# A gated S5 and SiLU-FFN layer on one core: C by DMA transposes, state slot 3 in pairs, four conversions on GpSimd

## The chip, the cores and the metric

The kernel runs on one core of one Trainium2 chip. The metric is the device time of one execution in microseconds. Before the change the median of three runs is 145.91 us (145.41 to 146.05). All times below are microseconds unless marked otherwise; times within an execution count from its first instruction.

## What is computed

One input `x` of 2048 tokens by 448 features goes through two branches, and a sigmoid gate per token mixes them. Branch A is a diagonal complex state-space layer (S5) with 448 states, branch B a feed-forward layer with 1792 hidden features:

```
g     = sigmoid(sum(x * gate_w))
Lbar  = exp(dt * Lam);  dt = exp(log_dt);  Lam = Lambda_re + i Lambda_im
Bu    = x @ (((Lbar - 1) / Lam)[:, None] * (B_re + i B_im)).T
h_t   = Lbar * h_{t-1} + Bu_t                 (over 2048 tokens)
a     = 2 * real(h @ (C_re + i C_im).T) + x * Dskip
b     = silu(x @ w1) @ w2
out   = g * a + (1 - g) * b
```

Inputs and output are bf16.

## The kernel before

**Chunks and slots.** Tokens are worked on in four chunks of 512 (`CH`), the readout in 16 blocks of 128 tokens. The 448 complex states make 896 real rows, kept in seven slots of 128 partitions: slots 0 to 2 hold the real parts of 384 states, 4 to 6 their imaginary parts, and slot 3 the real parts of the last 64 states above their imaginary parts. Before, the 384 states of slots 0 to 2 are interleaved (state 3p + s stands in partition p of slot s), so that a load of B reads three neighbouring rows of DRAM into each partition; C's columns and the parameters are then taken with a stride of 3.

**The complex scan as a real one.** `lanes(tc)` turns each chunk's inputs U by the phase of every state and time (products with COS and SIN on DVE), runs a real scan with decay `rc` on DVE for each slot (L670), converts each result Gf to bf16 (Gb, L673, on ScalarE, ACT below) and turns it back (products at L657), which gives H for the readout. A slot's partner is the slot 4 away; slot 3's partner is its own other half, which a DMA within SBUF swaps into row 7 of U and Gb (`swapped`, L636; in chunk 0 two DVE copies, L653, for U). COS and SIN of 512 times are made at the start for four blocks of states: the phase is multiplied by the time (L493 on ACT for blocks 0 and 1, L496 on GpSimd for 2 and 3), brought into the range of the sine by subtracting the nearest whole turn (`nearest`, `minus`, DVE), and put through ACT's sine. Eight columns of sines at the end of a chunk (s8, c8, L524 to L526) serve the carry between chunks (CC, SS, gin) and, over a row of small GpSimd instructions (L529), the scales `sc1` and `sc2` that turn C into the scaled readout weights CP.

**PE's work.** TensorE (PE) multiplies x by B for U (`bu_pair`, and `bu_last` for slot 3, L644), by w1 for the hidden layer (`ffn1_pair`), the hidden layer by w2 (`ffn2`, L706), and H by CP (`readout`, L731). The contraction over 448 features is 3.5 times 128. `step` takes two outputs at once, one fed from the upper 64 rows of the array and one from the lower: seven matmuls of half height for each output, in a `begin` of 8 and an `end` of 6 (L595). The end of a pair is issued after the begin of the next. `bu_last` does slot 3 with four matmuls of full height, the last padded with zeros (L799). ACT or DVE empties the result from one of eight PSUM banks: U (L622, L624), the SiLU (L695), Tb = (1 - g) b (L710). DVE adds the branches up in `readout` (tf at L725, ot at L734), and a DMA on SyncE's queue (SP) writes each block of 128 rows.

**The start and C.** x of chunk 0, B and C come as they lie in DRAM and are transposed by PE with the identity matrix (L435, L569, L747), x of chunks 1 to 3 by DMA transposes (L369). PE runs 15 idle matmuls (L420) while x arrives. The parameters (Lambda, log_dt, gate_w: `prm`, four rows) are copied once by DVE (L453) and brought into columns by PE (L459, L461).

**Order.** Engines issue in order. PE's order is the order of the calls at the end of the kernel, written out by hand. For the other engines and the DMA queues a planner (`Plan.order`) simulates the program with a cost and a priority for each operation and picks the next one that could start. `Waits` turns the dependences into semaphore waits. PSUM banks are handed out by the planner too.

Of the kernel before, what the change touches and what calls it, by code (L numbers as in the profile page):

```python
# [7 lines left out]
ALU = mybir.AluOpType  # L8
# [253 lines left out]
def bass_gated_mix__ssm_conv_s5__dense_activation_silu__prompt_kernel(nc, A_x, A_Lambda_re, A_Lambda_im, A_B_re, A_B_im, A_C_re, A_C_im,  # L262
               A_log_dt, A_Dskip, B_x, B_w1, B_w2, gate_w, out):
    with ExitStack() as ctx:
# [25 lines left out]
        Cnat = Tb[0:112, 7:16, :].rearrange("p a b -> p (a b)")[:, 0:3840].rearrange("p (b l) -> p b l", b=4)  # L290
# [13 lines left out]
        prm = sb("prm", [4, 512], BF16)  # L304
# [68 lines left out]
        load("sp", Bnat[:, 0:3, :], A_B_re[0:384, :].rearrange("(p s) d -> p s d", s=3), "Bn0", 384 * 896, 1)  # L373
        load("sp", Bnat[:, 4:7, :], A_B_im[0:384, :].rearrange("(p s) d -> p s d", s=3), "Bn3", 384 * 896, 2)
# [12 lines left out]
        load("sp", Cnat[:, :, 0:448], A_C_re.rearrange("(b p) l -> p b l", p=112), "Cn0", 448 * 896, 11)  # L387
        load("sp", Cnat[:, :, 576:960], A_C_im[:, 0:384].rearrange("(b p) l -> p b l", p=112), "Cn1", 448 * 768, 12)
        load("sp", Cnat[:, :, 448:512], A_C_im[:, 384:448].rearrange("(b p) l -> p b l", p=112), "Cn2", 448 * 300, 13)
        load("sp", Cnat[:, :, 512:576], A_C_re[:, 384:448].rearrange("(b p) l -> p b l", p=112), "Cn3", 448 * 300, 14)  # L390
# [36 lines left out]
        def x_transposes(n):  # L427
            tk = Ps()

            def mm(pe):  # L430
                for q in range(2):
                    i = 2 * n + q
                    for b in range(4):
                        o = (q * 4 + b) * 128
                        r = pe.transpose(bk16(tk)[:, o:o + 128], xnat[:, b, XCOL[i]:XCOL[i] + 128], ident[:, :])  # L435
                return r
            P.add("pe", mm, ["xn0", "ident"], [tk], 0.5)
            if n == 0:
                DVE(lambda e: e.tensor_copy(xT[:, 0:2, 0:CH], bk16(tk)[:, :].rearrange("p (q n) -> p q n", q=2)),
                    [tk], ["xT00"], 0.7, 2)  # L440
            else:
                ACT(lambda e: e.activation(xT[:, 2, 0:CH], bk16(tk)[:, 0:CH], AF.Copy), [tk], ["xT01"], act_cost(512), 1)
                DVE(lambda e: e.tensor_copy(xT[:, 3, 0:CH], bk16(tk)[:, CH:2 * CH]), [tk, "xT01"], ["xT02"], 0.42, 2)

        x_transposes(0)
        x_transposes(1)

        def xr(tc):
            return [f"xT{tc}{k}" for k in range(2 if tc else 3)]


        prmn = [f"prm{k}" for k in range(4)]
        DVE(lambda e: e.tensor_copy(prm[:, 448:512], prm[:, 384:448]), prmn, ["prmd"], 0.2, 1)  # L453
        tk = Ps()

        def prm_t(pe, tk=tk):
            for b in range(4):
                lanes = prm[0:4, b:384:3] if b < 3 else prm[0:4, 384:512]
                pe.transpose(bk16(tk)[:, 4 * b:4 * b + 4], lanes, ident[0:4, 0:4])  # L459
            for b in range(3):  # L460
                r = pe.transpose(bk16(tk)[:, 16 + 4 * b:16 + 4 * b + 4], prm[0:4, 128 * b:128 * b + 128], ident[0:4, 0:4])  # L461
            return r
        P.add("pe", prm_t, prmn + ["prmd", "ident"], [tk], 0.3)
        DVE(lambda e, tk=tk: e.tensor_copy(
            pc[:, :, :], bk16(tk)[:, 0:16].rearrange("p (b k) -> p k b", k=4)), [tk], ["pc"], 0.2, 1)
        DVE(lambda e, tk=tk: e.tensor_copy(
            gwc[:, 0:3], bk16(tk)[:, 16:28].rearrange("p (b k) -> p k b", k=4)[:, 3, :]), [tk], ["gwc"], 0.2, 4)
        POOL(lambda e: e.tensor_copy(gwc[:, 3:4], pc[:, 3, 3:4]), ["pc"], ["gwc3"], 0.2, 15)
# [20 lines left out]
        for b in range(4):  # L489
            q = b % 2  # L490
            dst = Gf[:, b, :]
            if b < 2:
                ACT(lambda e, b=b, dst=dst: e.activation(dst, itf[:, :], AF.Copy, scale=ph[:, b:b + 1]),  # L493
                    ["itf", "ph"], [f"Gf{b}"], act_cost(512, 1), 2)
            else:
                POOL(lambda e, b=b, dst=dst: e.tensor_single_scalar(dst, itf[:, :], ph[:, b:b + 1], ALU.mult),  # L496
                     ["itf", "ph"], [f"Gf{b}"], 1.65)
            DVE(nearest(wk[q], dst), [f"Gf{b}"], [f"Gf{4 + q}"], dve_cost(512, 2), 3)
            DVE(minus(dst, dst, wk[q]), [f"Gf{b}", f"Gf{4 + q}"], [f"Gf{b}"], dve_cost(512), 3)
# [59 lines left out]
        def b_transposes(slots, reads, h, to_act):  # L559

            tk = Ps()
            n = len(slots)

            def mm(pe):
                for q in range(2):
                    i = 2 * h + q
                    for j, s in enumerate(slots):
                        o = (q * n + j) * 128
                        r = pe.transpose(bk16(tk)[:, o:o + 128], Bnat[:, s, XCOL[i]:XCOL[i] + 128], ident[:, :])  # L569
                return r  # L570
            P.add("pe", mm, reads + ["ident"], [tk], 0.06 * 2 * n)
            dst = BT[:, 2 * h:2 * h + 2, slots[0] * 128:(slots[-1] + 1) * 128]
            src = lambda: bk16(tk)[:, 0:2 * n * 128].rearrange("p (q m) -> p q m", q=2)
            name = f"BT{h}_{slots[0]}"
            if to_act:
                ACT(lambda e: e.activation(dst, src(), AF.Copy), [tk], [name], act_cost(256 * n), 0)
            else:
                DVE(lambda e: e.tensor_copy(dst, src()), [tk], [name], 0.1 + 0.00058 * 256 * n, 0)

        B01, B23, B456 = (0, 1), (2, 3), (4, 5, 6)  # L580
        b_transposes(B01, ["Bn0"], 0, False)
        b_transposes(B01, ["Bn0"], 1, True)
        idle(2)
        b_transposes(B456, ["Bn3"], 0, False)
        b_transposes(B456, ["Bn3"], 1, True)
        b01, b23, b456 = ([f"BT{h}_{s}" for h in range(2)] for s in (0, 2, 4))
# [4 lines left out]

        def half_steps(pe, w, xc, a, b, lo, hi, start):
            for i in range(len(lo)):
                for p0, (tk, c0), k in ((0, a, lo[i]), (64, b, hi[i])):
                    r = pe.matmul(bk(tk), w[p0:p0 + 64, k, c0:c0 + 128], xT[p0:p0 + 64, k, xc:xc + CH],  # L595
                                  start=(start and i == 0), stop=(not start and i == 2))
# [4 lines left out]
        def step(pair):  # L601

            w, tc, ca, cb, reads, evict = pair
            a, b = Ps("pair"), Ps("pair")
            xc = tc * CH
            begin = lambda pe: half_steps(pe, w, xc, (a, ca), (b, cb), (0, 1, 2, 3), (0, 1, 2, 3), True)
            end = lambda pe: half_steps(pe, w, xc, (b, cb), (a, ca), (0, 1, 2), (0, 1, 3), False)
            reads = reads + xr(tc)
            P.add("pe", begin, reads, [a, b], 0.87, rows=64)
# [8 lines left out]


# [6 lines left out]
        def bu_pair(tc, k):  # L626
            sa, sb_ = ((0, 1), (4, 5), (6, 2))[k]

            def evict(a, b):
                u_out(sa, a)  # L630
                u_out(sb_, b, tc == 0)
            return BT, tc, 128 * sa, 128 * sb_, (b01, b456, b456 + b23)[k], evict
# [5 lines left out]

        def bu_last(tc):
            tk = Ps()  # L640

            def mm(pe):
                for i in range(4):
                    r = pe.matmul(bk(tk), BT[:, i, 384:512], xT[:, i, tc * CH:(tc + 1) * CH],  # L644
                                  start=(i == 0), stop=(i == 3))
                return r
            P.add("pe", mm, b23 + ["BT3z"] + xr(tc), [tk], 0.87)
            u_out(3, tk)
            if tc:
                swapped(U, "U", 0)  # L650
            else:
                for k, p in ((0, 0), (1, 64)):
                    DVE(lambda e, p=p: e.tensor_copy(U[p:p + 64, 7, :], U[64 - p:128 - p, 3, :]),  # L653
                        ["U3"], [f"U7{'ab'[k]}"], dve_cost(512, 4), 2)
# [4 lines left out]
        def lanes(tc):  # L659
# [7 lines left out]
            for s in (3, 0, 4, 1, 5, 2, 6):  # L667
# [5 lines left out]
                ACT(lambda e, s=s: e.activation(Gb[:, s, :], Gf[:, s, :], AF.Copy), [f"Gf{s}"], [f"Gb{s}"], act_cost(512), 4)  # L673
# [18 lines left out]
        def ffn1_pair(tc, k):  # L692
            def evict(a, b):
                for tk, fb in ((a, k), (b, 7 + k)):
                    ACT(lambda e, tk=tk, fb=fb: e.activation(aT[tc % 2][:, fb, :], bk(tk), AF.Silu),  # L695
                        [tk, "tbl"], [f"aT{tc % 2}_{fb}"], act_cost(512), 3)
            part = 0 if k < 3 else 1
            return w1s, tc, 128 * k, 896 + 128 * k, [f"w1{part}{n}" for n in range(5)], evict

        def ffn2(tb):  # L700
# [3 lines left out]
            def mm(pe, tk=tk):  # L704
# [4 lines left out]
            P.add("pe", mm, ["w2"] + [f"aT{tc % 2}_{fb}" for fb in range(NFB)], [tk], 2.66)  # L709
            ACT(lambda e, tk=tk: e.activation(Tb[:, tb, :], bk(tk)[:, 0:D_MOD], AF.Copy, scale=g1[:, tb:tb + 1]),  # L710
                [tk, f"g1_{tc}"], [f"Tb{tb}"] + [f"{'B' if tb < 7 else 'C'}n{k}" for k in range(4)], act_cost(448, 1), 3)
# [8 lines left out]
        def readout(tb):  # L720
            tc, o = tb // 4, (tb % 4) * 128
            t0 = tb * 128
            tk = Ps("C")
# [174 lines left out]
```

## Time and profile before

| What | us |
|---|---|
| Median of the runs | 145.91 |
| Profiled execution, its own time | 145.11 |
| Its span, first to last instruction | 143.3 |
| Half-height matmuls on B (L595), 168 | 19.7 busy |
| Half-height matmuls on w1 (L595), 392 | 43.8 busy |
| Hidden layer by w2 (L706), 224 matmuls | 44.7 busy |
| Readout (L731), 112 matmuls | 23.1 busy |
| DVE scans (L670), 21 of chunks 1 to 3 | 25.8 busy |
| ACT conversions Gb (L673), 28 | 17.2 busy |
| GpSimd scalings of 512 columns (L496), 2 | 3.1 busy |

The granted TensorE clock is 1.0 in the whole execution. A group of the profile is named by line, engine, operation and tile; its busy time is the sum of the durations of its instructions. Matmuls are pipelined, so that the duration of one (0.38 us at L595) is longer than the distance from one to the next; distances are read from the chain of waits, which gives start, length and count of each stretch. DMA issues on SP and ACT are not counted as busy.

### The profile page before, as it was taken

The numbers are of one execution on the slowest core, as the hardware profiler recorded it, in microseconds if no ns is written. First come the engines' busy times: TensorE is split into PE (matmuls) and PEld (weight loads), VectorE is DVE, ScalarE is ACT, GpSimd is POOL, SyncE is SP. The second block draws the span as 40 slices with busy tenths as digits, with TensorE's granted clock in tenths as the row PEclk, the third lists the DMA queues.
The fourth block names the chain that finished last, engine by engine and source line by source line (L and its number), as shares of the span: only waits on it lengthen the run. The fifth ranks groups of instructions, "written<-read, shape, count | busy, mean of one in ns | idle before, by whom it ended". The sixth has DMA issues, their size and how long they took to land.

```text
span 143.3 us, 2726 instructions
## 1 busy us (share of the span) xinstructions
PE 138.5 (97%) x1076; PEld 69.3 (48%) x1076; DVE 123.9 (86%) x144; ACT 82.6 (58%) x154; POOL 25.3 (18%) x62
## 2 busy tenths in 40 slices
PE   6899999999999999999999999999999999999991
PEld 4744543444446654444555554444455555555550
DVE  0459979999999999999799999969479999889592
ACT  3298799799778466978921134978811344411100
POOL 7176960000601300023170000040000000000000
PEclk9999999999999999999999999999999999999999
DMA  4999979015987000000011002000020021000022
GB/s 145 311 252 263 327 140 236 2 37 121 180 204 250 5 0 19 17 0 5 0 39 64 20 17 69 0 0 5 0 69 32 0 73 32 32 18 16 32 92 71
DMA packets 18165, 11.44 MB, mean 80 GB/s; under 512 B 8036, under 2 KB 17896, under 8 KB 18152
## 3 DMA queue, kind: packets, MB, share of 16 engines
q1 hardware_dynamic: 18144, 11.27, 31.1%
q8 instruction: 8, 0.13, 0.4%
q14 instruction: 5, 0.04, 0.1%
q10 hardware_dynamic: 8, 0.00, 0.0%
HBM read 6.94 MB, written 1.84 MB: 61 GB/s over the span
## 4 chain that ended last, share of the span: by engine, by line
PE 91%; ACT 5%; DVE 2%; issue 0%; DVEq 0%
PE ps L595 37%; PE ps L706 30%; PE ps L731 15%; PE ps L644 3%; PE ps L420 2%; ACT aT L695 2%; ACT COS L512 1%; PE ps L569 1%; PE ps L747 1%; PE ps L770 1%; PE ps L435 1%; DVE Gf L482 0%; DVE ot L734 0%; ACT SIN L507 0%; DVE U L653 0%
## 5 line engine op out<-in xcount | busy, mean ns | idle before, releaser
L706 PE MATMUL ps<-w2s,aT 128*128 128x448 bf16 x224 | 44.7, 353 | 0.0
L595 PE MATMUL ps<-xT,w1s 64*128 64x512 bf16 x392 | 43.8, 376 | 0.3 <-ACT aT L695 0.3
L695 ACT ACTIVATE aT<-ps 128x512 bf16<-128x512 f32 x56 | 29.6, 598 | 5.1 <-PE ps L595 5.1
L706 PEld LDWEIGHTS ps<-w2s,aT 128*128 128x128 bf16 x224 | 21.7, 98 | 20.4 <-issue 0.4
L595 PEld LDWEIGHTS ps<-xT,w1s 64*128 64x128 bf16 x392 | 18.9, 94 | 23.5 <-ACT aT L695 1.6
L710 ACT ACTIVATE Tb<-ps,g 128x448 bf16<-128x448 f32 x16 | 10.1, 633 | 32.6 <-PE ps L706 26.6
L670 DVE TENSOR_TENSOR_SCAN Gf<-rc,gin,PA 128x512 f32<-128x512 f32 x21 | 25.8, 1269 | 0.0
L731 PE MATMUL ps<-CP,H 128*128 128x448 bf16 x112 | 23.1, 353 | 0.0
L595 PE MATMUL ps<-xT,BT 64*128 64x512 bf16 x168 | 19.7, 377 | 0.0
L673 ACT ACTIVATE Gb<-Gf 128x512 bf16<-128x512 f32 x28 | 17.2, 628 | 3.8 <-DVE Gf L670 3.8
L624 ACT ACTIVATE U<-ps 128x512 bf16<-128x512 f32 x25 | 14.2, 596 | 3.2 <-PE ps L595 2.8
L734 DVE SCALAR_TENSOR_TENSOR ot<-ps,g,tf 128x448 bf16<-128x448 f32 x16 | 10.8, 677 | 6.0 <-PE ps L731 5.9
L731 PEld LDWEIGHTS ps<-CP,H 128*128 128x128 bf16 x112 | 10.9, 98 | 10.1
L595 PEld LDWEIGHTS ps<-xT,BT 64*128 64x128 bf16 x168 | 7.9, 94 | 10.1 <-ACT Tb L710 0.4
L679 POOL TENSOR_TENSOR k<-Gf,CC 128x7 f32<-128x7 f32 x3 | 2.8, 927 | 50.5 <-DVE Gf L670 50.5
L725 DVE SCALAR_TENSOR_TENSOR tf<-xnat,g,Tb 128x448 f32<-128x448 bf16 x16 | 10.7, 676 | 0.3
L657 DVE TENSOR_TENSOR PB<-Gb,SIN 128x1536 bf16<-128x1536 bf16 (+1 forms) x8 | 8.7, 1086 | 2.5 <-ACT Gb L673 2.3
L657 DVE TENSOR_TENSOR PB<-U,SIN 128x2048 bf16<-128x2048 bf16 (+1 forms) x8 | 8.4, 1083 | 0.1
L657 DVE TENSOR_TENSOR PA<-U,COS 128x3584 bf16<-128x3584 bf16 x4 | 8.1, 2018 | 0.1
L657 DVE TENSOR_TENSOR H<-PA,PB 128x3584 bf16<-128x3584 bf16 x4 | 8.1, 2026 | 0.1
L657 DVE TENSOR_TENSOR PA<-PA,PB 128x3584 bf16<-128x3584 bf16 x4 | 8.1, 2018 | 0.0
L657 DVE TENSOR_TENSOR PA<-Gb,COS 128x3584 bf16<-128x3584 bf16 x4 | 8.1, 2018 | 0.0
(98 smaller groups left out, 100.8 us busy)
## 6 DMA issues: line engine op xcount, KB each, us to landing
xnat<-in_A_x_dram SPq DMA_DIRECT2D x4, 448.0 KB, 4.8
out_dram<-ot SPq DMA_DIRECT2D x16, 112.0 KB, 1.7
w2s<-in_B_w_dram SPq DMA_DIRECT2D x1, 1568.0 KB, 9.9
w1s<-in_B_w_dram SPq DMA_DIRECT2D x3, 256.0 KB, 5.1
w1s<-in_B_w_dram SPq DMA_DIRECT2D x3, 192.0 KB, 4.4
Gb<-Gb SPq DMA_DIRECT2D x8, 64.0 KB, 1.9
Tb<-in_A_C_re_dram SPq DMA_DIRECT2D x1, 392.0 KB, 4.4
U<-U SPq DMA_DIRECT2D x6, 64.0 KB, 2.0
```

The source lines that it names most:

```text
L595: r = pe.matmul(bk(tk), w[p0:p0 + 64, k, c0:c0 + 128], xT[p0:p0 + 64, k, xc:xc + CH], start=(start and i == 0), stop=(not start and i == 2))
L624: ACT(lambda e: e.activation(U[:, s, :], bk(tk), AF.Copy), [tk], [f"U{s}"], act_cost(512), 4)
L644: r = pe.matmul(bk(tk), BT[:, i, 384:512], xT[:, i, tc * CH:(tc + 1) * CH], start=(i == 0), stop=(i == 3))
L657: return DVE(lambda e: e.tensor_tensor(o, a, b, op), r, w, dve_cost(n, 2), prio)
L670: DVE(lambda e, s=s, b=b, init=init: e.tensor_tensor_scan(Gf[:, s, :], rc[:, b:b + 1].to_broadcast([128, CH]), PA[:, s, :], init, ALU.mult ...
L673: ACT(lambda e, s=s: e.activation(Gb[:, s, :], Gf[:, s, :], AF.Copy), [f"Gf{s}"], [f"Gb{s}"], act_cost(512), 4)
L695: ACT(lambda e, tk=tk, fb=fb: e.activation(aT[tc % 2][:, fb, :], bk(tk), AF.Silu), [tk, "tbl"], [f"aT{tc % 2}_{fb}"], act_cost(512), 3)
L706: r = pe.matmul(bk(tk)[:, 0:D_MOD], aT[tc % 2][:, fb, o:o + 128], w2s[:, fb, :], start=(fb == 0), stop=(fb == NFB - 1))
L710: ACT(lambda e, tk=tk: e.activation(Tb[:, tb, :], bk(tk)[:, 0:D_MOD], AF.Copy, scale=g1[:, tb:tb + 1]), [tk, f"g1_{tc}"], [f"Tb{tb}"] + [f ...
L725: DVE(lambda e: e.scalar_tensor_tensor(tf[tb % 2][:, :], xnat[:, tb, :], g[:, tb:tb + 1], Tb[:, tb, :], ALU.mult, ALU.add), [f"xn{tc}", f" ...
L731: r = pe.matmul(bk(tk)[:, 0:D_MOD], Ht[:, s, o:o + 128], CP[:, s, :], start=(s == 0), stop=(s == NSLOT - 1))
L734: DVE(lambda e, tk=tk: e.scalar_tensor_tensor(ot[tb % 3][:, :], bk(tk)[:, 0:D_MOD], g[:, tb:tb + 1], tf[tb % 2][:, :], ALU.mult, ALU.add), ...
```

## The change

The diff has these parts.

1. **Natural order of the states.** State 128 s + p stands in partition p of slot s. B is loaded with three runs of one row for each partition, and the parameters are transposed without a stride; gate_w's columns come out of the same transposes, and the copy of prm goes.
2. **The start.** x of chunk 0 is transposed in four groups of four (before two of eight), each emptied by one DVE or ACT instruction. The parameters are transposed first, then B's slots 0 and 1; B's slots 4 to 6 come behind the first B matmuls, and the gates of chunk 0 behind B's last transposes. In chunk 0 DVE empties four U slots.
3. **Phases.** Blocks 0 and 1 do without ACT's scaling: DVE makes the nearest turn in two instructions and the rest in a third.
4. **Slot 3 in pairs.** `step` takes any two outputs, with weights and chunk of their own; slot 3 is paired with an FFN block, and some FFN blocks with one of the next chunk. `bu_last` and the zeroing go.
5. **GpSimd.** In chunks 1 and 2 it converts Gb of slots 0 and 1.
6. **C.** Two DMA transposes bring 384 columns of C_re and C_im; the last 64 columns come in three small loads and are transposed by PE. ACT and DVE read the scaled C's sources from SBUF.
7. **The last readout** is done in two halves of 224 columns, each with its own eviction and DMA.

The costs given to the planner and some priorities change with them. The core of the diff:

```diff
-        load("sp", Bnat[:, 0:3, :], A_B_re[0:384, :].rearrange("(p s) d -> p s d", s=3), "Bn0", 384 * 896, 1)
+        load("sp", Bnat[:, 0:3, :], A_B_re[0:384, :].rearrange("(s p) d -> p s d", p=128), "Bn0", 384 * 896, 1)
...
-        load("sp", Cnat[:, :, 0:448], A_C_re.rearrange("(b p) l -> p b l", p=112), "Cn0", 448 * 896, 11)
-        load("sp", Cnat[:, :, 576:960], A_C_im[:, 0:384].rearrange("(b p) l -> p b l", p=112), "Cn1", 448 * 768, 12)
...
+            P.add("sp", lambda e: e.dma_start_transpose(dst, src), [], [f"Cn{k}"], cost, prio, sem(), 448 * 800)
...
+        load_ct(0, CT[:, 0:3, :], A_C_re[:, 0:384], 2.0, 11)
+        load_ct(1, CT[:, 3:6, :], A_C_im[:, 0:384], 2.0, 12)
+        for k, src in enumerate((A_C_re, A_C_im, A_C_re)):
+            load("sp", Cnat[:, :, 64 * k:64 * k + 64], src[:, 384:448].rearrange("(b p) l -> p b l", p=112), f"Cn{2 + k}", 448 * 300, 13 + k)
...
-        DVE(lambda e: e.tensor_copy(prm[:, 448:512], prm[:, 384:448]), prmn, ["prmd"], 0.2, 1)
...
+        P.add("pe", prm_t, prmn + ["ident"], [tk], 0.3)
+        b_transposes(B01, ["Bn0"], 0, False)
+        b_transposes(B01, ["Bn0"], 1, True)
+        idle(2)
...
             if b < 2:
-                ACT(lambda e, b=b, dst=dst: e.activation(dst, itf[:, :], AF.Copy, scale=ph[:, b:b + 1]),
-                    ["itf", "ph"], [f"Gf{b}"], act_cost(512, 1), 2)
+                DVE(lambda e, b=b, t=t: e.tensor_scalar(t, itf[:, :], ph[:, b:b + 1], ROUND, ALU.mult, ALU.add),
+                    ["itf", "ph"], [f"Gf{4 + q}"], dve_cost(512, 2), 3)
+                DVE(lambda e, t=t: e.tensor_single_scalar(t, t, -ROUND, ALU.add), [], [f"Gf{4 + q}"], dve_cost(512, 2), 3)
+                DVE(lambda e, b=b, t=t, dst=dst: e.scalar_tensor_tensor(dst, itf[:, :], ph[:, b:b + 1], t, ALU.mult, ALU.subtract),
+                    ["itf", "ph", f"Gf{4 + q}"], [f"Gf{b}"], dve_cost(512), 3)
...
-        def step(pair):
+        def step(ta, tb):
 
-            w, tc, ca, cb, reads, evict = pair
+            (wa, xa, ca, ra, ea), (wb, xb, cb, rb, eb) = ta, tb
             a, b = Ps("pair"), Ps("pair")
...
+            begin = lambda pe: half_steps(pe, (wa, xa, a, ca), (wb, xb, b, cb), (0, 1, 2, 3), (0, 1, 2, 3), True)
+            end = lambda pe: half_steps(pe, (wb, xb, b, cb), (wa, xa, a, ca), (0, 1, 2), (0, 1, 3), False)
...
+        GP = ((), (0, 1), (0, 1), ())
...
+                u_out(s, tk, tc == 0 and s in (1, 2, 5, 6))
...
+                if s in GP[tc]:
+                    POOL(lambda e, s=s: e.tensor_copy(Gb[:, s, :], Gf[:, s, :]), [f"Gf{s}"], [f"Gb{s}"], 0.75, 8)
+                else:
+                    ACT(lambda e, s=s: e.activation(Gb[:, s, :], Gf[:, s, :], AF.Copy), [f"Gf{s}"], [f"Gb{s}"], act_cost(512), 4)
...
+            for c in ((slice(0, D_MOD),) if tb + 1 < NTB else (slice(0, 224), slice(224, D_MOD))):
...
+                re, im = (lambda: CT[:, k, :]), (lambda: CT[:, 3 + k, :])
+                src = ["Cn0", "Cn1"]
...
-        BU(0, 0)
+        BU(0, (0, 1))
+        b_transposes(B456, ["Bn3"], 0, False)
+        b_transposes(B456, ["Bn3"], 1, True)
         b_transposes(B23, ["Bn0", "Bn1", "Bn2"], 0, False)
         b_transposes(B23, ["Bn0", "Bn1", "Bn2"], 1, True)
...
+        BU(0, (4, 5), (6, 2))
+        step(bu(0, 3), f1(0, 7))
+        F1(0, (0, 8), (1, 9), (2, 10), (3, 11), (4, 12), (5, 13))
...
+        step(f1(0, 6), f1(1, 13))
+        F1(1, (1, 7), (2, 8))
         close()
         F2(0)
-        bu_last(1)
...
+        step(f1(1, 0), bu(1, 3))
+        BU(1, (0, 1), (4, 5), (6, 2))
+        F1(1, (3, 9), (4, 10), (5, 11), (6, 12))
...
+        step(bu(2, 3), f1(2, 7))
...
+        step(f1(2, 6), f1(3, 13))
+        step(f1(3, 0), bu(3, 3))
```

## The prediction

> **What bounds the kernel now.** I read the engines' busy shares first, then the chain of waits in order of time, then the timelines of PE, DVE, ACT and GpSimd around the places that the change touches, and last the landings of the DMAs. From the page, busy time with the shares of the chain, and from the list of waits all that PE matmuls waited for:
>
> ```profile
> PE 138.5 (97%) x1076; PEld 69.3 (48%) x1076; DVE 123.9 (86%) x144; ACT 82.6 (58%) x154; POOL 25.3 (18%) x62
> ...
> PE 91%; ACT 5%; DVE 2%; issue 0%; DVEq 0%
> ...
> PE ps L420 <- DVE PB L413: 1.2, 1, 1.2
> PE ps L459 <- DVE prm L453: 0.5, 1, 0.5
> PE ps L595 <- ACT aT L695: 0.3, 1, 0.3
> ```
>
> PE is the bound: after the start it waits 0.8 us in all. So a matmul that goes away is worth its whole duration, unless another engine then comes last. The chain in order of time (start, length, what) gives the price of every kind of PE work:
>
> ```profile
> 5.55 0.17 DVE prm L453
> ...
> 9.14 4.67 PE ps L595 x42
> 13.81 0.98 PE ps L644 x4
> ...
> 32.76 0.86 PE ps L644 x4
> ...
> 44.79 0.81 PE ps L747 x16
> 45.60 2.65 PE ps L706 x14
> 48.25 0.79 PE ps L747 x16
> ...
> 54.33 15.22 PE ps L595 x140
> 69.55 0.97 PE ps L644 x4
> ...
> 102.42 0.97 PE ps L644 x4
> ...
> 133.85 6.63 PE ps L731 x35
> 140.48 0.03 DVEq L256
> 140.52 0.04 issue
> 140.56 0.68 DVE ot L734
> ```
>
> Half-height matmuls (L595) run at 15.22/140 = 0.1087 us each, full-height 512-column ones (L644) at 0.24, the C transposes (L747) at 0.05. The second engine is DVE, 86% busy, without a gap over 0.2 us from 21 to 68; only its last product H(3) (130.39 to 132.41) has a near deadline: readout 12 starts at 133.85 + 1.32 = 135.17, so it has 2.76 us to spare.
>
> **Term 1, C by DMA.** 32 PE transposes (0.81 + 0.79 = 1.60) become 8 (0.40): **-1.20**. Two plain loads of 392 and 336 KB (issues 0.58 and 0.48, landed 25.4 at the latest) become two DMA transposes, and the two small loads become three. The nearest row is the x transpose of 1024 x 384, issued in 3.05 and landed in 5.7; 448 rows are 0.44 of it, so 1.3 us of SP each. The far bound is the first x transpose: 7.96 to issue behind w2's traffic, landed after 10.8. SP would finish at 19.9 + 2.6 + 3 x 0.5 = 24 (far bound 37) instead of 22.1. Behind them on SP stands only the Gb swap of chunk 0, free at 28 to 30 and needed by DVE at 36, and behind that x of chunks 2 and 3, needed by PE at 52. DVE first reads C at 44.6. I cost the DMAs at nothing; that cover ends where C lands after 44, and at the far bound DVE would wait 3 for the swap, inside the margin found below.
>
> **Term 2, slot 3 in pairs.** The four groups at L644 cost 0.98 + 0.86 + 0.97 + 0.97 = 3.78. Half-height, slot 3 takes 7 matmuls a chunk, 28 x 0.1087 = 3.04: **-0.74**. In chunk 0 the 42 half-height matmuls took 4.67 where 42 x 0.1087 is 4.57; that 0.10 is the price of one change of height, and one round trip less in chunk 0 gives **-0.10** (bounds 0 and 0.2). A pair that mixes w1 and B columns has the shape of the others; I price it alike.
>
> **Term 3, the start.** DVE's copy of prm goes and with it PE's wait of 0.51 and two of seven small transposes (0.05). The parameters' last load landed at 4.97 (its semaphore in the trace), PE asks for it at 5.37, so nothing takes its place there. But the 12 transposes of B456, which stood between the transposes of B01 and the first B matmuls, now stand behind them. PE after: x transposes end 5.37, parameters 5.62, B01 6.17, two idle matmuls 6.39. ACT has two x evictions (0.60 each, from 4.97 to 6.1), then the exponential (0.20), then B01's eviction (0.60), which ends at 6.85. PE's first B matmul starts at 6.9: a new wait of 0.5. Then 8 matmuls 7.9, B456 8.55, B23 9.1, gates 9.57. Before, the same work without gates ended at 9.14, and gates cost 0.48: 9.62. Sum of the term **-0.05** (bounds -0.5, if ACT is in time, and +0.4). GpSimd makes gwc by about 7, ahead of the gates. The B loads change from 2,688-byte to 896-byte runs; the x load has 896-byte runs and landed 448 KB in 3.3, so B_re (landed 4.86, asked for at 5.62) and B_im (6.55, asked for at 7.9) stay covered; uncovered, each us late is a us of PE.
>
> **Term 4, chunk 0's evictions.** PE's 0.3 wait came from eight banks full of FFN results while ACT had done two scalings (1.32), SIN and COS. The scalings leave ACT; the three sines of eight columns (0.7) move to later gaps; U5, U6, U1, U2 are now DVE's (four at 0.69; before three). DVE gets six passes of 512 columns where it had four for blocks 0 and 1: 2 x (0.42 + 0.42 + 0.69). I put DVE's U6 and U2 at 16.5 and PE's need of their banks at 17.2; ACT's eviction of FFN block 9 ends 21.35 and the bank is asked for at 21.7. So **-0.32**, with margins of only 0.4 to 0.7; bounds -0.32 and +0.7 (the passes at 0.69 each would be that much late). Chunk 1's x is asked for at 23.3; it landed at 21.96.
>
> **Term 5, the end.** The last readout in two halves: PE 14 x 0.095 = 1.32, as before. The last eviction of 224 columns takes, between 0.17 for 16 columns (L464) and 0.68 for 448, 0.42: **-0.25**. The last DMA: 112 KB rows landed in 1.7; bounds -0.3 and +0.9 (the slowest of 16 took 2.6); I take 0.
>
> On that DMA the Trainium skill, "DMA: Bandwidth & Descriptors", section Specifications, speaks against the change: under 512 bytes a transfer is below line rate, and the halves have 448-byte rows. By that rule half the bytes gain nothing, by the row alone some 0.1; no run so far shows it.
>
> **GpSimd's conversions and the late sines.** Four of ACT's 28 conversions (0.63 each) go; ACT is not the bound there, so nothing is gained. On GpSimd a 512-column conversion took 0.61 alone (L409), a 512-column scaling 1.56 beside DVE. What GpSimd pays beside DVE's two-input products:
>
> ```profile
> 36.04 0.83 POOL L679 TENSOR_TENSOR k<-Gf,CC 128x7 f32<-128x7 f32 x1 [15.79 <-DVE Gf L670]
> 36.83 0.19 POOL L680 TENSOR_TENSOR k<-Gf,SS 128x3 f32<-128x3 f32 x1
> ```
>
> 0.83 ends with DVE's product (35.88 to 36.81), the next takes 0.19: GpSimd waits for DVE. The sine c8 now stands behind evictions of chunk 1 on ACT, at about 41.15, and 16 GpSimd instructions follow until sc2, which the scaled C needs. Three wait for DVE's products (41.5 to 44.65). Then DVE itself waits at the first CP, GpSimd is free, and 11 more at 0.2 give sc2 at 46.85 and CP at 47.4. DVE loses 2.75 us; behind sc2 ACT holds the last two FFN evictions of chunk 1, whose banks PE wants only after 52.
>
> DVE's count: scans of chunk 0 from 26.6 (28.04 before, the U and Gf chain being shorter); H(0) 41.5; CP 47.4; H(1) 73.2; H(2) 101.0, as before (101.1). Now U3 comes early, so chunk 3 goes straight on: products 2.04 + 2.1 + 2.04, seven scans 8.3, products 2.1 + 2.04 + 2.06, nine evictions and sums at 0.6, and 1.9 of waiting for readouts give H(3) at 129.0. PE reaches readout 12 at 132.8. Margin 3.7, so **0**; if each GpSimd copy holds up a scan by 0.6 to 1.56 (2.4 to 6.2 in all), 0 to +2.5.
>
> The skill's "SBUF — State Buffer", section Who interferes with whom, says that a DVE instruction with two SBUF inputs and a GpSimd one that reads SBUF exclude each other for the whole instruction, whichever was first. The row shows only GpSimd losing; by the rule the scans lose up to 4 x 0.61 = 2.4 us as well, an estimate, still inside the margin.
>
> **Sum.** -1.20 - 0.74 - 0.10 - 0.05 - 0.32 - 0.25 = -2.66, rounded -2.6. The profiled execution had 143.3 of span in 145.11 in all: after, 140.7 in 142.5. The median of the runs lies 0.8 above that execution: 145.91 - 2.6 = **143.3**.
>
> **Rivals.** *Chunk 0 stalls.* For it: bank margins under 0.7, and DVE's added passes on the very chain that held PE before. Against: ACT is 1.32 + 0.7 lighter there. PE waits 1.0 in place of gaining 0.32: 143.3 + 1.3 = 144.6.
>
> *Slower: the scales of C come too late.* sc2 needs 16 dependent GpSimd instructions; the row above gives 0.83 for one beside DVE, and gin took 1.20. At 1.0 each sc2 comes at 57 and CP at 57.8, so DVE loses 13 instead of 2.75, 10.4 more, and H(3) at 139.4 is 6.6 behind PE: 149.9. It decides from 3.7 us of further delay, and the kernel is slower from 6.3. Against it: DVE, once it waits for CP, no longer disturbs GpSimd.
>
> *GpSimd holds the scans*, the upper bound above: +2.5, 145.8, no change.
>
> *Slot 3 does not pair*: if mixed pairs ran their two halves one after the other, 56 matmuls would cost 0.1087 more each, 6.1: 149.4. Against: before, too, the two halves used different weight columns and banks.
>
> **How the numbers follow.** Forecast 0.70; chunk 0 stalls 0.12; GpSimd holds the scans 0.05; scales too late 0.10; no pairing 0.03. A measurement here can't tell 0.5% (0.7 us). The first two are faster; of the third 0.04 is no change and 0.01 slower; of the late scales 0.03 end within 0.5%. Faster 0.82, same 0.07, slower 0.11. The range runs from 142.5 (the start and the last DMA at their good bounds) to 145.0 (chunk 0's rival and its margin).
>
> **What would show it.** Right: no group of L644's kind, 8 transposes at the C line, PE busy near 136.5, readouts C(12) to C(15) following without a wait. Step 3 wrong: no wait before the first B matmul, or one for a load. Term 4 wrong: PE waiting for ACT or DVE between 14 and 28. Scales wrong: the first CP after 51, and PE waiting for H ahead of readout 12.

## The result and the profile after

The changed kernel takes 144.00 us in the median (143.91 to 144.24), the kernel before 146.06 (145.41 to 146.28; six executions, with the three given at the start): a ratio of 0.9872, 95% interval 0.9856 to 0.9888, or 2.06 us less. The forecast was 143.3 with a range of 142.5 to 145.0, from a before of 145.91: 2.6 less. The sign holds; half a microsecond of the gain is missing.

First the lines of the page (busy times; shares of the chain) that answer to those shown of before,

```profile
PE 137.6 (97%) x1069; PEld 70.6 (50%) x1069; DVE 126.1 (89%) x145; ACT 79.1 (56%) x148; POOL 34.2 (24%) x66
...
PE 96%; DVE 1%; ACT 1%; POOL 1%; issue 0%
```

and of the list of waits (who waits for whom; us in total, times, longest):

```profile
PE ps L425 <- DVE PB L418: 1.2, 1, 1.2
PE ps L599 <- DVE ph L511: 0.6, 1, 0.6
PE ps L599 <- ACT BT L475: 0.2, 1, 0.2
```

PE carries 96% of the chain (91% before) and waits for nobody after the start. The chain of waits (start, length, what) gives the price of each stage; lines have moved: matmuls of half height are L599 now, C's transposes L751, the gates L774, the readout L731.

```profile
4.56 1.71 PE ps L441 x16
...
7.90 1.02 PE ps L599 x8
8.92 0.79 PE ps L468 x12
...
9.74 0.82 ACT BT L475
...
10.69 18.95 PE ps L599 x174
...
47.75 0.40 PE ps L751 x8
...
53.44 15.37 PE ps L599 x140
68.81 0.89 PE ps L774 x32
...
85.61 16.72 PE ps L599 x154
102.33 1.43 PE ps L731 x7
...
139.57 0.45 DVE ot L735
```

Three readings. The group of full-height matmuls on B is gone, and 174, 140 and 154 matmuls of half height follow each other at 0.109 to 0.110 us. C's transposes are 8 in 0.40. The last eviction takes 0.45 instead of 0.68.

The first line is not an effect of the change. The same 16 transposes of x took 0.91 us in the profiled execution of before (0.057 each) and take 1.71 here (0.107 each): in this execution PE's clock doubled only at their end, in that of before just ahead of them, though the granted clock is given as 1.0 in both pages. The Trainium skill, "TensorE: Matmul & The Clock Gate", Part 1, has the two distances (106.7 and 55.6 ns for 128 columns) and says that the gate's window runs freely, so that the moment differs from run to run; the rows agree. The idle matmuls ahead of them start at 1.18 in both; the transposes end at 5.37 before and at 6.27 now. So 0.9 us of a single profile is chance here: the two spans, 143.3 and 142.0, differ by 1.3 only, and with 0.9 put back by 2.2, close to the 2.06 of the medians. Stages below are compared behind that point.

Two more readings, of the timeline of GpSimd (start, length, instruction, idle time before and what ended it):

```profile
42.30 0.40 POOL L584 COPY CC<-c 128x4 f32<-128x4 f32 x1 [6.69 <-ACT c L559]
...
42.79 2.03 POOL L585 COPY CC<-c 128x3 f32<-128x3 f32 x1
44.79 1.22 POOL L565 TENSOR_SCALAR cw<-cw 128x4 f32<-128x4 f32 x1
...
47.82 0.24 POOL L583 TENSOR_SCALAR sc<-cw 128x4 f32<-128x4 f32 x1
...
58.48 1.51 POOL L669 CAST Gb<-Gf 128x512 bf16<-128x512 f32 x1 [6.11 <-DVE Gf L665]
```

A copy of three columns takes 2.03 us while a product of DVE runs beside it, where its neighbours take 0.2. So the scales of C end at 48.06, six us after the sine. The timeline of ScalarE shows who stands behind them:

```profile
43.99 1.08 ACT L692 ACTIVATE aT<-ps 128x512 bf16<-128x512 f32 x2 [0.42 <-PE ps L599]
48.17 0.67 ACT L757 ACTIVATE ct<-Tb,sc 128x448 f32<-128x448 bf16 x1 [3.10 <-POOL sc L583]
...
64.77 2.07 ACT L692 ACTIVATE aT<-ps 128x512 bf16<-128x512 f32 x4
66.68 0.68 ACT L671 ACTIVATE Gb<-Gf 128x512 bf16<-128x512 f32 x1
67.20 3.08 ACT L692 ACTIVATE aT<-ps 128x512 bf16<-128x512 f32 x6
```

ACT stands idle for 3.10 at the first ct, and DVE for 3.07 at the first CP (48.98). From 62 to 70 ACT runs without a gap, behind PE. In this execution the list shows no wait of PE for it, but 140 matmuls take 15.37 where 15.21 is their pace: the margin is used up.

### The profile page after: what moved, and what is told of

Its sections match the earlier page's. It is cut to its first block, busy times and chain, and to the rows that moved or that the text cites. A ratio compares the mean times of both kernels' runs of the same rounds, so it can differ in the third digit from the quotient of the medians.

```text
span 142.0 us, 2706 instructions
## 1 busy us (share of the span) xinstructions
PE 137.6 (97%) x1069; PEld 70.6 (50%) x1069; DVE 126.1 (89%) x145; ACT 79.1 (56%) x148; POOL 34.2 (24%) x66
## 4 chain that ended last, share of the span: by engine, by line
PE 96%; DVE 1%; ACT 1%; POOL 1%; issue 0%
PE ps L599 45%; PE ps L703 30%; PE ps L731 15%; PE ps L425 2%; PE ps L441 1%; PE ps L774 1%; ACT BT L475 1%; PE ps L468 1%; POOL cw L562 0%; DVE ot L735 0%; PE ps L751 0%; DVE PB L418 0%; POOL gwc L497 0%; DVE pc L495 0%; DVE cw L570 0%
## 5 line engine op out<-in xcount | busy, mean ns | idle before, releaser
L599 PE MATMUL ps<-xT,w1s 64*128 64x512 bf16 x392 | 47.4, 376 | 0.0
L599 PEld LDWEIGHTS ps<-xT,w1s 64*128 64x128 bf16 x392 | 21.0, 94 | 22.7 <-issue 0.7
L665 DVE TENSOR_TENSOR_SCAN Gf<-rc,gin,PA 128x512 f32<-128x512 f32 x21 | 26.8, 1322 | 0.0
L599 PE MATMUL ps<-xT,BT 64*128 64x512 bf16 x196 | 25.9, 376 | 0.7 <-DVE ph L511 0.6
L731 PE MATMUL ps<-CP,H 128*128 128x448 bf16 (+1 forms) x119 | 23.2, 341 | 0.0
L671 ACT ACTIVATE Gb<-Gf 128x512 bf16<-128x512 f32 x24 | 14.7, 630 | 8.4 <-DVE Gf L665 8.3
L599 PEld LDWEIGHTS ps<-xT,BT 64*128 64x128 bf16 x196 | 10.7, 94 | 12.1 <-DVE phk L508 0.8
L731 PEld LDWEIGHTS ps<-CP,H 128*128 128x128 bf16 x119 | 11.5, 98 | 9.8 <-issue 0.4
L633 ACT ACTIVATE U<-ps 128x512 bf16<-128x512 f32 x24 | 13.3, 592 | 2.2 <-PE ps L599 2.2
L735 DVE SCALAR_TENSOR_TENSOR ot<-ps,g,tf 128x448 bf16<-128x448 f32 (+1 forms) x17 | 11.1, 650 | 3.2 <-issue 2.2
L669 POOL CAST Gb<-Gf 128x512 bf16<-128x512 f32 x4 | 6.1, 1518 | 23.0 <-DVE Gf L665 23.0
```

Source lines behind the costliest of these rows:

```text
L633: ACT(lambda e: e.activation(U[:, s, :], bk(tk), AF.Copy), [tk], [f"U{s}"], act_cost(512), 4)
L665: DVE(lambda e, s=s, b=b, init=init: e.tensor_tensor_scan(Gf[:, s, :], rc[:, b:b + 1].to_broadcast([128, CH]), PA[:, s, :], init, ALU.mult ...
L669: POOL(lambda e, s=s: e.tensor_copy(Gb[:, s, :], Gf[:, s, :]), [f"Gf{s}"], [f"Gb{s}"], 0.75, 8)
L731: r = pe.matmul(bk(tk)[:, 0:n], Ht[:, s, o:o + 128], CP[:, s, c], start=(s == 0), stop=(s == NSLOT - 1))
L735: DVE(lambda e, tk=tk, c=c, n=n: e.scalar_tensor_tensor(ot[tb % 3][:, c], bk(tk)[:, 0:n], g[:, tb:tb + 1], tf[tb % 2][:, c], ALU.mult, ALU ...
```

## The experiments

The changed kernel is called *after* here. Differences against it, or between two experiments, are of ratios to the kernel before in the same session, times 146 us; the intervals of the two ratios are put together as the root of the sum of squares.

### One part undone at a time

**C by TensorE transposes again.** Two plain loads, and all four groups of C go through PE and PSUM:

```diff
-            P.add("sp", lambda e: e.dma_start_transpose(dst, src), [], [f"Cn{k}"], cost, prio, sem(), 448 * 800)
...
+        load("sp", CN[:, :, 0:384], A_C_re[:, 0:384].rearrange("(b p) l -> p b l", p=112), "Cn0", 448 * 768, 11)
...
+            tk = Ps()
```

> The changed kernel with C's 384 columns loaded as they lie and transposed by PE (32 transposes in place of 8), all else as changed. If PE's work is the bound throughout, the 24 transposes at 0.050 come back whole: 144.0 + 1.2 = 145.2 us. Rival, the DMA transposes cost something elsewhere (SP's queue, the swap of chunk 0): less than 1.2 comes back, 144.6 or below.

Measured: 146.45 (145.81 to 147.03), ratio 1.0056 (1.0034 to 1.0078): 2.7 ± 0.4 above *after*, twice the transposes' 1.2. PE's list of waits has 0.9 for ScalarE's aT in chunk 2, and the chain there goes from GpSimd's cw through CP, the scans and Gb to that aT.

**Slot 3 at full height again**, in all four chunks; of the edit, chunk 0:

```diff
-        step(bu(0, 3), f1(0, 7))
-        F1(0, (0, 8), (1, 9), (2, 10), (3, 11), (4, 12), (5, 13))
+        F1(0, (0, 7))
+        bu_last(0)
+        F1(0, (1, 8), (2, 9), (3, 10), (4, 11), (5, 12), (6, 13))
...
```

> The changed kernel with slot 3 again in four full-height matmuls per chunk and the FFN pairs as before, all else as changed. Theory of the prediction: the pairing is worth 0.84, 144.85 us. The stretches of the two profiled executions give less, 1.84 + 1.94 before against 1.37 + 1.66 after and 0.22 lost where gates and the first readout behind a pair now pay the change of height: 0.53, 144.5 us. Rival, mixed pairs cost more than pure ones: no loss, 144.0 us or below.

Measured: 145.07 (144.53 to 145.88), ratio 0.9961 (0.9942 to 0.9979): 1.3 ± 0.4 above *after*, and again PE waits for ScalarE (U 0.5, aT 0.3).

**B456 ahead of the first B matmuls**, as before the change:

```diff
+        b_transposes(B456, ["Bn3"], 0, False)
+        b_transposes(B456, ["Bn3"], 1, True)
...
         BU(0, (0, 1))
-        b_transposes(B456, ["Bn3"], 0, False)
-        b_transposes(B456, ["Bn3"], 1, True)
```

> The changed kernel with B456's 12 transposes again ahead of the first B matmuls, where they cover the eviction of B01. If the two waits of 0.56 and 0.17 in the start are the price of that order, they go: 144.0 - 0.6 = 143.4 us. Rival, ACT's table load and its evictions are behind the B matmuls in any order: 143.9 to 144.1.

Measured: 143.41 (142.66 to 143.66), ratio 0.9829 (0.9804 to 0.9853): 0.6 ± 0.4 better. The wait of 0.56 before the first B matmul is gone, and BU(4,5), the matmuls of x by B for slots 4 and 5, starts at 10.04 instead of 10.69 in two executions whose x transposes ran alike (1.66 and 1.71).

**No conversions on GpSimd.**

```diff
-        GP = ((), (0, 1), (0, 1), ())
+        GP = ((), (), (), ())
```

> The changed kernel with all conversions on ACT, none on GpSimd. GpSimd's four copies lengthen four DVE scans from 1.26 to 1.56, 1.2 us of DVE, but H(3) is ready 2 to 3 us ahead of its readout: no change, 143.9 to 144.1 us, and H(3) about 1 us earlier. Rival, the four conversions relieve ACT where PE waits for it: slower, 144.5 us or more.

Measured: 144.86 (144.56 to 145.33), ratio 0.9940 (0.9918 to 0.9962): 1.0 ± 0.4 above *after*, where the forecast had the four conversions at nothing. The chain of this execution says how; from its list, by order of time:

```profile
41.10 0.20 ACT c L559
...
41.91 1.97 POOL CC L585
43.88 1.19 POOL cw L565
...
46.91 0.21 POOL sc L583
...
47.23 0.68 ACT ct L757
...
48.04 0.68 DVE CP L761
...
56.27 5.91 DVE Gf L665 x5
...
62.21 0.63 ACT Gb L671
62.84 0.98 ACT aT L692 x2
...
63.87 5.35 PE ps L599 x48
```

From the sine of the scales at 41.10 to a matmul at 63.87 there is one unbroken chain off PE. GpSimd's 16 small instructions hold ct on ACT, CP on DVE, and with them chunk 1's scans; their conversions then meet the evictions of chunk 2 on ACT, and PE waits for a bank. PE began BU(4,5) 0.95 earlier than in *after*, as its clock doubled earlier, and reached the gates of chunk 2 at 69.22, 0.41 later.

So three different parts, undone, each cost more than their own price, and each time PE waited for ScalarE in chunk 2. That gave a new theory: the *late scales* are the hidden cost, just covered in *after* and uncovered by whatever starts earlier or loads ACT more. The rival is that the parts are simply worth what these runs showed.

### The scales earlier

**Sine and absolute value at once.** Their priority in the plan goes from 12 to 3.5:

```diff
-        ACT(lambda e: e.activation(s8[:, :], ph[:, :], AF.Sin, scale=TURN), ["ph", "ph5", "tbl"], ["s8"], 0.25, 12)
+        ACT(lambda e: e.activation(s8[:, :], ph[:, :], AF.Sin, scale=TURN), ["ph", "ph5", "tbl"], ["s8"], 0.25, 3.5)
...
-        ACT(lambda e: e.activation(c8[:, :], pha[:, :], AF.Sin, bias=hpi[:, :], scale=-TURN), ["pha", "hpi", "tbl"], ["c8"], 0.3, 12)
+        ACT(lambda e: e.activation(c8[:, :], pha[:, :], AF.Sin, bias=hpi[:, :], scale=-TURN), ["pha", "hpi", "tbl"], ["c8"], 0.3, 3.5)
```

It was run alone, with B456 early, with slot 3 at full height, and with C on PE.

> The changed kernel with the second sine and its absolute value on ScalarE right behind the one before them (priority 12 to 3.5), so that the scales of C are ready some 10 us earlier. Late-scales theory (ScalarE and TensorE of chunk 2 run at their edge because C's scales, ct and CP come late): TensorE waits for nothing of ScalarE in chunk 2, first CP before 42 us, median 143.0 to 143.7, and the runs spread like those of before (0.7 and more). Rival (the scales bind nothing): 143.9 to 144.1, as the changed kernel. Second rival (the three ScalarE instructions, done earlier, stop an eviction of chunk 0): 144.3 to 144.6, with a TensorE wait for ScalarE between 25 and 32 us.

> The early scales and B456 ahead of the first B matmuls together. Late-scales theory: both gains add, 142.4 to 143.1. Rival (the scales bind nothing): 143.2 to 143.5, as with B456 early alone (143.41).

> The early scales with slot 3 at full height again: the price of the pairs without late scales in the way. Late-scales theory: 0.5 to 0.85 above the run with early scales alone (the traces of before and after gave 0.53, the prediction 0.84), so about 143.9 to 144.3. Rival (pairs are worth 1.1 to 1.3 in themselves, as undoing them alone showed): 1.1 to 1.3 above it.

> The early scales with C by TensorE transposes again. Late-scales theory: the 24 transposes alone come back, 1.2 above the run with early scales, about 144.4 to 144.9. Rival (the way of C costs 2.5 in itself: the transposes' PSUM banks and ScalarE or VectorE evictions count too): 2.3 to 2.7 above it.

Measured: alone 151.47 (150.40 to 152.27), ratio 1.0396 (1.0361 to 1.0432); with B456 151.47, ratio 1.0387 (1.0346 to 1.0429); with slot 3 152.41, ratio 1.0455 (1.0424 to 1.0485). All three expectations were wrong by 8 us; only the third's distance from the first, 0.9 ± 0.7, fits what it expected, and its rival too. Only the one with C on PE came out as the late scales have it: 144.75, ratio 0.9930 (0.9907 to 0.9953).

Of the run with early scales alone, the line of PE's waits that is new:

```profile
PE ps L599 <- ACT U L633: 5.7, 1, 5.7
```

its busy times by stretch (stretch; length; busy time and instructions of PE, PEld, DVE, ACT, POOL; granted clock; DMA share; GB/s):

```profile
36.30:42.78 6.48, 0.79 (x8) 0.18 (x5) 5.65 (x10) 6.48 (x13) 2.19 (x4) 0.94 0.63 127
42.78:46.20 3.42, 3.42 (x20) 1.34 (x22) 3.42 (x3) 2.29 (x5) 0.00 (x0) 0.61 0.18 43
46.20:53.00 6.80, 6.80 (x70) 3.25 (x67) 5.60 (x5) 4.98 (x11) 0.46 (x1) 1.00 0.79 218
```

and two lines of its timeline of ScalarE, one of DVE's:

```profile
30.15 0.32 ACT L559 ACTIVATE c<-pha,hpi 128x8 f32<-128x8 f32 x1
...
36.23 0.67 ACT L757 ACTIVATE ct<-Tb,sc 128x448 f32<-128x448 bf16 x1 [2.88 <-POOL sc L583]
```

```profile
37.03 0.68 DVE L761 SCALAR_TENSOR_TENSOR CP<-Tb,sc,ct 128x448 bf16<-128x448 bf16 x1 [3.95 <-ACT ct L757]
```

The sine is 11.8 us earlier than in *after* (0.8 of that is the clock's start, which came early here), but the plan counts 0.1 to 0.15 for each GpSimd instruction and therefore put ct and CP in front of chunk 0's conversions and its last scan. Beside the scans such instructions took 1.1 to 1.2 (28.60 to 33.08 for four of them), and the scales came at 36.12. ACT and DVE, which issue in order, stood still, the evictions of U behind them too, and PE waited 5.7. On top of that its clock was lower, 0.61 granted in the 3.42 behind the wait: 62 matmuls behind the wait took 8.15 where 6.74 is their pace. 5.7 + 1.4 = 7.1 of the 7.3 by which this span exceeds the next experiment's. It is the rival "the scales of C come too late", brought about in another place. With C on PE, CP needs PE's transposes, which stand behind chunk 1's products in PE's order, so its readers stayed late and nothing was blocked.

**Scales early, readers late.** The same edit, and in the plan alone the last scale counts 10 us; ct and CP are back where *after* has them:

```diff
-        POOL(lambda e: e.tensor_single_scalar(sc2[:, :], a3, -1.0, ALU.mult), ["a3"], ["sc2"], 0.1, 20)
+        POOL(lambda e: e.tensor_single_scalar(sc2[:, :], a3, -1.0, ALU.mult), ["a3"], ["sc2"], 10, 20)
```

It was run alone, with B456 early, with slot 3 at full height, and without conversions on GpSimd.

> The changed kernel with c8 early (priority 3.5) and, in the plan alone, sc2 put down as 10 us long, so that ct and CP keep the places they have in the changed kernel: the scales are ready some 10 us earlier and nobody is queued behind them in chunk 0. Late-scales theory: no wait of TensorE for ScalarE behind the start, no 5.7 us wait in front of chunk 1's evictions, median 143.0 to 143.7 (the run with early scales and C on TensorE, 144.75, less the 1.2 of the transposes is 143.55), runs spread over 0.7 and more like those of before. Rival (the scales bind nothing in the changed kernel): 143.9 to 144.1 and as tight as it.

> The same with B456 ahead of the first B matmuls. Late-scales theory: 0.6 below the run before it, 142.4 to 143.1. Rival (the scales bind nothing): 143.2 to 143.5, as B456 early alone (143.41).

> Early scales with their readers in late places, and slot 3 at full height again: the price of the pairs with no late scales in the way. Late-scales theory: 0.5 to 0.85 above the run with early scales alone (the traces of before and after gave 0.53, the prediction 0.84). Rival (the pairs are worth 1.1 to 1.3 in themselves): 1.1 to 1.3 above it.

> Early scales with their readers in late places, and all conversions of lanes on ScalarE again, none on GpSimd. Late-scales theory (ScalarE was short only because of ct and the late scales): within 0.3 of the run with early scales alone, and no wait of TensorE for ScalarE. Rival (the four conversions relieve ScalarE in chunks 1 and 2 in any case): 0.7 to 1.0 above it, with TensorE waits for U or aT between 55 and 100 us.

| Experiment | Median | Ratio to before | 95% interval |
|---|---|---|---|
| Scales early, readers late | 143.43 | 0.9831 | 0.9808 to 0.9853 |
| and B456 early | 142.96 | 0.9798 | 0.9776 to 0.9820 |
| and slot 3 at full height | 144.46 | 0.9890 | 0.9867 to 0.9913 |
| and no conversions on GpSimd | 143.28 | 0.9827 | 0.9803 to 0.9851 |

Of the first, the chain in chunk 2,

```profile
52.56 15.21 PE ps L599 x140
67.77 0.89 PE ps L774 x32
```

and a line each of the timelines of DVE and of ScalarE:

```profile
44.01 0.68 DVE L761 SCALAR_TENSOR_TENSOR CP<-Tb,sc,ct 128x448 bf16<-128x448 bf16 x1
```

```profile
64.15 1.08 ACT L692 ACTIVATE aT<-ps 128x512 bf16<-128x512 f32 x2 [0.43 <-PE ps L599]
```

CP comes at 44.01 without a wait of DVE, ACT waits for PE again, not PE for ACT, and 140 matmuls take their 15.21. Against *after* the median is 0.6 ± 0.4 lower. The conversions on GpSimd are worth nothing now (-0.1 ± 0.5, rival 0.7 to 1.0): in the earlier run they were worth 1.0 only because the late scales had made ACT short. Slot 3 in pairs is worth 0.9 ± 0.5 and C by DMA 1.4 ± 0.5 (the run with C on PE against the first line). The spread of 0.5 was below the 0.7 expected; four runs say little of it.

For slot 3 the interval reaches to the rival's 1.1 to 1.3 too; the chains of the profiled executions decide. BU(4,5) starts in each of them behind the moment at which the clock doubled; from there to the end of the last matmul PE took:

| Profiled execution | BU(4,5) starts | Last matmul ends | Between |
|---|---|---|---|
| *after* | 10.69 | 139.54 | 128.85 |
| C on PE | 9.76 | 141.11 | 131.35 |
| slot 3 at full height | 9.83 | 140.19 | 130.36 |
| no conversions on GpSimd | 9.74 | 139.96 | 130.22 |
| scales early, readers late | 9.81 | 138.51 | 128.70 |
| scales early and C on PE | 10.80 | 140.68 | 129.88 |
| scales early, readers late, and slot 3 at full height | 10.56 | 139.91 | 129.35 |
| scales early, readers late, and no conversions | 10.71 | 139.41 | 128.70 |

With late scales the three parts are worth 2.50, 1.51 and 1.37; with early scales 1.18, 0.65 and 0.00. So in these three the late scales add 1.32, 0.86 and 1.37, and without them each part is worth its price on PE (1.20 for C, 0.68 for the pairs, nothing for the conversions).

B456 early adds 0.5 ± 0.5 to the early scales and brings the best version: 142.96, 1.1 ± 0.4 below *after* and 2.0% below the kernel before.

How much the late scales cost *after* itself is not settled. In the table it is 0.15, the 15.37 against 15.21 of chunk 2. The 0.6 ± 0.4 of the medians holds the clock's start too: the spans of *after*'s six executions are 141.9 to 142.3, all like the profiled one, whose clock doubled late; the four with early scales have 141.2 (the profiled one, with an early clock), 141.2, 141.9 and 141.7. Either all six of *after* had a late clock, or those with an early clock lost to the late scales what they had gained. For the second speaks only how much the six are alike. Against it speaks the run without conversions, whose clock doubled early: sine, scales and first CP come 0.95 earlier than in *after* (40.99 against 41.94 for the sine, 48.04 against 48.98 for CP), as BU(4,5) does, so that their chain moves along with PE. And the run with B456 early, with the same late scales, has a span of 141.4 with a late clock, in its profile, and one of 140.6 among its others. No profile of *after* with an early clock was taken.

## Why the prediction was right, and where not

**C by DMA, -1.20:** right. 1.60 became 0.40 in the chain; by the table it is worth 1.18 with early scales, by the medians 1.4 ± 0.5. The DMAs cost nothing: the two transposes were issued in 1.33 and 1.79 (estimate 1.3) and landed by 25.1, and the swap of chunk 0 left at 31.6.

**Slot 3 in pairs, -0.74, and -0.10 for a change of height:** the mechanism was right, the size a little off. By the chain chunks 0 and 1 gave 0.47 and chunks 2 and 3 0.43 (with 15.21 for *after*'s 15.37), but two changes of height moved instead of going: gates of chunks 2 and 3 now take 0.89 (0.78 before) and the first readout behind a pair 1.43 (1.32). That is 0.68 instead of 0.84; by the table above it is 0.65. "Slot 3 does not pair" fell with the pace of 0.109.

**The start, -0.05:** it was +0.17. The wait of 0.5 before the first B matmul came as forecast (0.56). The list of waits names DVE's phase for it, which happened to end at that moment; the matmul reads B01, whose second eviction ACT ends at 7.74. Missed was a second wait, 0.17 for B456's eviction, which ACT begins only at 9.74. Putting B456 back brought 0.6: the step cost what the copy of prm had cost.

**Chunk 0's evictions, -0.32:** right; 174 matmuls in 18.95 without a wait. The rival "chunk 0 stalls" fell.

**The end, -0.25:** about -0.36. From PE's last matmul to the end of the span it is 2.46 now and was 2.82. The eviction gave 0.23 of it, and the halves of 56 KB landed no slower than whole rows:

```profile
out_dram<-ot SPq DMA_DIRECT2D x15, 112.0 KB, 1.7
...
out_dram<-ot SPq DMA_DIRECT2D x2, 56.0 KB, 1.5
```

The rule that spoke against short rows (the Trainium skill, "DMA: Bandwidth & Descriptors", Specifications) does not show in these two transfers.

**GpSimd's conversions and the late sines, 0:** this step was incomplete. Its clockwork was right: sine 41.15 (41.94), scales 46.85 (48.06), first CP 47.4 (48.98), DVE idle 2.75 (3.07), and H(3), the H of the last chunk, at 130.1 against readout 12 at 134.2, a margin of 4. The rival "scales too late" asked for that margin too, so it did not come. But both asked only DVE and the end. The sentence "whose banks PE wants only after 52" looked at the two evictions directly behind ct; it did not follow ACT on into chunk 2, where 3.1 idle, seven ct and the conversions that chunk 1's late scans push back meet U's and the hidden layer's evictions. In the profiled execution that cost 0.15; in the timed ones at most the 0.6 ± 0.4 above. "ACT is not the bound there" held for *after* only thanks to the four conversions: without them, and with the scales late, PE loses 1.37.

**GpSimd and the scans:** each conversion took 1.51 instead of 0.61, and the scan behind it 1.56 instead of 1.26: 0.30 for each, 1.2 in all, inside the margin. The Trainium skill's rule of exclusion ("SBUF — State Buffer", Who interferes with whom) agrees in that DVE loses too; the prediction's estimate by it, 0.61 each, was twice the measured price.

The missing half microsecond has no single source. The terms as measured are -1.20 - 0.68 + 0.17 - 0.32 - 0.36 = -2.39, and with the 0.15 lost to the late scales -2.24; the profiled spans differ by 2.2 with the clock's start taken out, the medians by 2.06. Against the forecast's sum of 2.66 the start is 0.22 short, the pairs 0.16 and chunk 2 0.15, and the end is 0.11 better.

## What to carry to other kernels

When a part of a change makes a value later, follow it through every in-order queue that reads it, past the first instruction behind it, to the next stage of the bounding engine; a margin at the end does not cover an engine that idles in the middle. Undoing parts one by one prices them wrongly where they share a hidden limit: two parts came out at twice their worth, and one at 1.4 us instead of nothing, until the limit was lifted. Profiles of single executions, compared from a point behind the clock's start, told apart what medians with intervals of 0.5 could not. And where a plan orders queues by estimated costs, earlier data can be worse than late: a reader placed by an estimate of 0.15 for instructions that take 1.1 to 1.2 cost 8 us.

## What the runs showed of the hardware that was not expected

- Two kernels with the same median (143.43 and 143.28) have profiled spans of 141.2 and 142.0. Their 16 x transposes took 0.99 and 1.71: a single profile's span holds up to 0.8 us of the clock's starting moment.
- Behind a wait of PE of 5.7 us in mid-kernel its granted clock was 0.61 over 3.4 us, which made the wait cost 7.1.
- GpSimd instructions of three or four columns last as long as the DVE product or scan beside them: 2.03 beside a product of 2.02, 1.16 beside scans of 1.13, 0.2 alone.
- A change between matmuls of half and of full height costs PE about 0.1 in the three places where the chain shows it: gates 0.89 instead of 0.78, the first readout behind a pair 1.43 instead of 1.32, the first block by w2 behind a pair 2.75 instead of 2.65.
